# Three partition sums as fp32r products of a split, and a new order around the key-value product

## The chip, the cores and the metric

The kernel runs on one NeuronCore of a Trainium2 chip. The metric is device time in microseconds (us). Before the change it is 570.62 us, the median of three runs (570.37 to 571.47).

The core's engines each work through a queue of their own in order: TensorE (PE in the profile; PEld is its weight load) multiplies matrices into PSUM, VectorE (DVE) and ScalarE (ACT) do elementwise work, GpSimd (POOL) a little of it, and SyncE (SP) issues the DMA transfers. They wait for each other through semaphores.

## The reference

A transformer block with adaptive layer norm, on one sequence of S = 2048 tokens of width D = 512, in float32:

```python
mod = (silu(c) @ w_mod).reshape(1, 6, 1, D)
sa, ca, ga, sb, cb, gb = (mod[:, i] for i in range(6))

h = layernorm(x) * (1 + ca) + sa
q, k, v = heads(h @ wqkv)                 # 32 heads of 16
phi = lambda t: where(t > 0, t + 1, exp(t)) + 1e-6
kv = sum over tokens of phi(k) outer v    # 16 x 16 for each head
z  = sum over tokens of phi(k)
o  = (phi(q) @ kv) / (phi(q) . z + 1e-6)
x  = x + ga * (o @ wo)

h = layernorm(x) * (1 + cb) + sb
x = x + gb * (((h @ w_gate) * (h @ w_up)) @ w_down)   # inner width 1376
```

## The kernel before, in words

**Precision.** TensorE works on fp32r operands. To keep float32 accuracy, `split` writes an operand as two fp32r tiles: ScalarE copies the high part, VectorE subtracts it from the operand for the low part. `product` then adds three matmuls for each contraction block: high times high, high times low, low times high. Two kinds of matmul take plain fp32 operands instead: the transposes by an identity, and sums over partitions by a matrix or column of ones.

**Tiling.** Tokens come in 4 chunks (NCH) of 4 tiles (NJ) of 128; a tile is 128 x 512. Widths are cut into KD = 4 blocks of 128. All working tiles in SBUF come from one pool of 99 buffers. PSUM has eight banks of 128 x 512 fp32: four in the pool `ps_acc`, taken by `acc_bank()`, and four in `ps_w`, taken by `bank()`. A new tile of a pool takes a bank whose last reader in the program has read it.

**Order.** The order of each engine's queue is the order in which the program calls the instructions (`manual_schedule`, line 37); nothing reorders them. The stages are:

1. The modulation vectors ca and sa, the norm of the first chunk, the first key projections (to line 391).
2. The key loop (lines 421 to 469), 16 steps i. In step i TensorE makes a projection two tiles ahead (`proj`, 12 matmuls), and adds to `tacc`, four accumulated banks, the products of phi(k) with the normalized tokens (`t_tile`, 12 matmuls). ScalarE and VectorE split the tiles of step i + 1 and compute phi(k) of step i + 2. VectorE adds phi(k) into `zacc` (`z_add`). What else must be done goes into the steps by a table, `extra` (lines 405 to 418): splits of projection weights, DMA loads of `w_mod` (`mod_load`), the modulation vectors 2 to 5 as weighted sums on VectorE (`mod_part`), which then are summed over partitions. Vectors 2 (ga) and 5 (gb) become rows repeated on all partitions (`mod_row`, line 174, in steps 11 and 15); 3 and 4 become columns. In step 12 the four blocks of `wo` are loaded (`raw_o`), in step 14 they are split (`wo_s`). In the last step `zacc` is summed over partitions (line 464) and ScalarE writes `zb` from it.
3. The joint (lines 529 to 567). ScalarE and VectorE scale `tacc` (lines 535, 536) and split it into `tt`. TensorE makes `kvps`, the product of the value weights `wv` with `tt` (lines 543 to 546): 48 matmuls of 128 x 128 into one bank. VectorE masks it to its head blocks (line 553) into `kvf`, which is split into `kvp`. `w_out(g)` (line 517) multiplies block g of `kvp` with `wo_s[g]`, three matmuls into a new bank; VectorE multiplies by ga into f, and f is split into `wp[g]`. Between these stand q projections 6 to 10: `proj`, then `q_a` (Relu and Exp on ScalarE), then `q_b` on VectorE, which reads the projection's bank last. `den_z`, `den_a` (a multiplication with zb and a sum for each tile), `den_b` (an addition and a reciprocal for a chunk) and `den_c` give the denominators of phi(q), all on VectorE.
4. The attention output tile by tile (`turn_a`, `y_step`), the second norm, and the feed-forward: three of its eleven blocks at first in the plain way, then the rest in a scheme with seven products instead of eight (from `ffn`, line 972). The first feed-forward loads (`load_ffn`, line 651, called at line 732) follow the joint in the program. Their first users are the splits at line 1031.

The joint's order of calls before, as far as TensorE is concerned, is: q projections 6 and 7, `kvps`, q projections 8 and 9, w_out(0) to (3), q projection 10. The three sums over partitions are:

```python
nc.tensor.matmul(ps, ones, acc, start=True, stop=True)      # line 176, twice
nc.tensor.matmul(zps, ones, zacc, start=True, stop=True)    # line 464
```

Of the kernel before, what the change touches and what calls it, by code (L numbers as in the profile page):

```python
# [9 lines left out]
F32R = mybir.dt.float32r  # L10
# [4 lines left out]
P = 128  # L15
# [7 lines left out]
def tile_adaln_block(  # L23
# [12 lines left out]
    nc = tc.nc  # L36
# [23 lines left out]
    consts = pool("consts", 1)  # L60
# [10 lines left out]
    def T(p, tag, shape=(P, D), dt=F32, bufs=None):  # L71
        cnt[0] += 1
        return p.tile(list(shape), dt, tag="t" if p is tiles else tag, name=f"{tag}_{cnt[0]}", bufs=bufs)

    def B(tag, shape=(P, D), dt=F32):

        return T(tiles, tag, shape, dt)
# [4 lines left out]
    def bank():  # L82
        return T(ps_w, "bank")
# [6 lines left out]
    ones = consts.tile([P, P], F32, name="ones")  # L90
# [17 lines left out]
    def load(src, tag):  # L108
        raw = B(tag, (P, *src.shape[1:]))[:src.shape[0]]
        nc.sync.dma_start(raw, src)  # L110
        return raw
# [4 lines left out]
    def load_mod(v):  # L116
        return [load(wm_v[:, k, v * D:(v + 1) * D], "raw") for k in range(KD)]
# [18 lines left out]
    idle_f = B("f")  # L136
    nc.vector.memset(idle_f, 0.0)
    nc.vector.tensor_copy(idle, idle_f)
    ps_idle = T(ps_acc, "acc")

    def keep_on(n):
# [14 lines left out]
    def mod_acc(acc, raws, ks):  # L156
        for k in ks:
            if k == 0:
                nc.vector.tensor_scalar(acc, raws[k], sc[:, 0:1], None, op0=ALU.mult)
            else:  # L160
                nc.vector.scalar_tensor_tensor(acc, raws[k], sc[:, k:k + 1], acc, op0=ALU.mult, op1=ALU.add)

    def mod_col(acc, ps):

        for b in range(KD):
            nc.tensor.matmul(ps[:, b:b + 1], acc[:, b * P:(b + 1) * P], ones[:, 0:1], start=True, stop=True)
        return ps

    def col_out(v, ps, add):
        t = consts.tile([P, KD], F32, name=f"col{v}")  # L170
        nc.vector.tensor_scalar(t, ps[:, :KD], add, None, op0=ALU.add)
        return t

    def mod_row(v, acc):
        ps = bank()
        nc.tensor.matmul(ps, ones, acc, start=True, stop=True)
        t = consts.tile([P, D], F32, name=f"row{v}")
        nc.scalar.activation(t, ps, AF.Copy)
        return t


    def split(src, h, l, low=None):
        nc.scalar.activation(h, src, AF.Copy)  # L183
        (low or nc.vector).tensor_tensor(l, src, f32(h), op=ALU.subtract)  # L184

    def split_raw(raw, shape=(P, D), low=None):
        h = B("w", shape, F32R)
        l = B("w", shape, F32R)
        split(raw, h[:raw.shape[0]], l[:raw.shape[0]], low)
        return h, l  # L190

    def product(ps, pairs):

        n = len(pairs)
        for i, ((ah, al), (bh, bl)) in enumerate(pairs):
            nc.tensor.matmul(ps, ah, bh, start=i == 0, stop=False)  # L196
            nc.tensor.matmul(ps, ah, bl, start=False, stop=False)  # L197
            nc.tensor.matmul(ps, al, bh, start=False, stop=i == n - 1)  # L198
# [11 lines left out]
    def cut(pair, a, b):  # L210
        return pair[0][:, a:b], pair[1][:, a:b]
# [67 lines left out]
    wk, wq, wv = [], [], []  # L279
    kx, phk, phq, q_ps = {}, {}, {}, {}  # L280

    def proj(i, w, of=bank):

        ch, j = divmod(i, NJ)
        ps = of()
        product(ps, [(cut(norm[ch].t[k], j * P, (j + 1) * P), w[k]) for k in range(KD)])
        return ps

    def phi_a(ps, t):

        nc.scalar.activation(t, ps, AF.Relu, scale=-1.0)
        nc.scalar.activation(t, t, AF.Exp, scale=-1.0)

    def phi_b(ps, t):
        nc.vector.scalar_tensor_tensor(t, ps, 0.0, t, op0=ALU.max, op1=ALU.add)
# [35 lines left out]
    def q_a(i, ps):  # L331
        phq[i] = B("h")
        q_ps[i] = ps
        phi_a(ps, phq[i])

    def q_b(i):
        phi_b(q_ps.pop(i), phq[i])

    zacc = B("z")
# [52 lines left out]
    rows, cols = {}, {}  # L392
    accs = {}

    raw_m, raw_o, wo_s = {}, [], []

    def mod_load(*vs):
        raw_m.update({v: load_mod(v) for v in vs})

    def mod_part(v, *ks):  # L400
        if 0 in ks:
            accs[v] = B("f")
        mod_acc(accs[v], raw_m[v], ks)
# [6 lines left out]
             6: lambda: (wv.extend(split_raw(r) for r in raw_v[2:3]), mod_load(2),),  # L410
             7: lambda: (wv.extend(split_raw(r) for r in raw_v[3:4]),),
             8: lambda: (mod_part(2, 0, 1), mod_load(3)),
             9: lambda: (mod_part(2, 2, 3), mod_load(4)),
             10: lambda: (mod_part(3, 0, 1, 2), mod_load(5)),
             11: lambda: (mod_part(3, 3), mod_part(4, 0, 1), rows.update({2: mod_row(2, accs[2])})),
             12: lambda: (raw_o.extend(load(wo_v[k], "raw") for k in range(KD)), mod_part(4, 2, 3), cols.update({3: col_out(3, mod_col(accs[3], bank()), 0.0)})),
             13: lambda: (mod_part(5, 0, 1, 2), cols.update({4: col_out(4, mod_col(accs[4], bank()), 1.0)})),
             14: lambda: (mod_part(5, 3), wo_s.extend(split_raw(x) for x in raw_o)), 15: lambda: rows.update({5: mod_row(5, accs[5])})}
    q_at = {3: 0, 4: 1, 6: 2, 7: 3}
    ahead = {2: proj(2, wk)}  # L420
    for i in range(NT):
        ch, j = divmod(i, NJ)
        more = ch + 1 < NCH
        if i == 0:
            ahead[3] = proj(3, wk)
        elif i > 1:
            ahead[i + 2] = proj(i + 2, wk) if i + 2 < NT else proj(i + 6 - NT, wq)
        if i in q_at:
            qps = proj(q_at[i], wq)
        if more and j == 0:  # L430
            nx.xhat(2)
        if i + 1 < NT:
            k_split_x(i + 1)
        if more and j == 0:
            nx.xhat(3)
        if i + 1 < NT:
            k_split(i + 1)
        if more and j < 2:
            t_tile(i, 0, 1)
            nx.transpose(2 * j, 2 * j + 1)  # L440
            nx.modulated(ca, sa, 2 * j, 2 * j + 1, cast=nc.vector)
            norm[ch + 1:] = [nx]
        if ch + 2 < NCH and j == 2:
            nx2 = Norm(xts[ch + 2])
            nx2.stats(0, 1)
        if ch + 2 < NCH and j == 3:
            nx = nx2
            nx.stats(2, 3)
            nx.rstd_of()
            nx.nmr_of()  # L450
            nx.xhat(0, 1)
        if i + 2 < NT:
            k_phi(i + 2, ahead.pop(i + 2))
        else:
            q_a(i + 6 - NT, ahead.pop(i + 2))
            q_b(i + 6 - NT)
        if i in q_at:
            q_a(q_at[i], qps)
            q_b(q_at[i])
        if i + 1 < NT:  # L460
            z_add(i + 1)
        if i == NT - 1:
            zps = bank()
            nc.tensor.matmul(zps, ones, zacc, start=True, stop=True)
            zb = consts.tile([P, D], F32, name="zb")
            nc.scalar.activation(zb, zps, AF.Identity, bias=eps_z)
        t_tile(i, *range(2 if more and j < 2 else 0, KD))
        if i in extra:
            extra[i]()
# [8 lines left out]
    def den_z():  # L478

        nc.vector.reduce_sum(den0, zb.rearrange("p (h i) -> p h i", i=DH), axis=AX.X)  # L480
        nc.vector.tensor_scalar(den0, den0, EPS_PHI, EPS_DEN, op0=ALU.mult, op1=ALU.add)

    def den_p(ch, *js, on=None):
        for j in js:
            pzs[ch, j] = B("f")
            (on or nc.gpsimd).tensor_tensor(pzs[ch, j], phq[ch * NJ + j], zb, op=ALU.mult)

    def den_r(ch, *js):
        if ch not in dens:
            dens[ch] = T(small, "den", (P, NJ, NH))  # L490
        for j in js:
            nc.vector.reduce_sum(dens[ch][:, j], pzs.pop((ch, j)).rearrange("p (h i) -> p h i", i=DH), axis=AX.X)

    def den_a(ch, *js, on=None):

        for j in js:
            den_p(ch, j, on=on)
            den_r(ch, j)
# [13 lines left out]
    def q_tile(i):  # L512
        q_a(i, proj(i, wq))
# [12 lines left out]
            wp.append((B("w", dt=F32R), B("w", dt=F32R)))  # L526
            split(f, *wp[-1])

    den_z()
    den_a(0, 0, 1, on=nc.vector)  # L530
    ps = proj(6, wq)
    fs, tt = [], []
    for k in range(KD):
        f = B("n")
# [3 lines left out]
    for f in fs:  # L538
        tt.append((B("w", dt=F32R), B("w", dt=F32R)))
        split(f, *tt[-1])  # L540
    q_a(6, ps)
    q_tile(7)
    kvps = bank()
    for g in range(KD):
        a, b = g * P, (g + 1) * P
        product(kvps[:, a:b], [(cut(wv[k], a, b), cut(tt[k], a, b)) for k in range(KD)])
    q_b(6)
    q_b(7)
    den_a(0, 2, on=nc.vector)
    ps = proj(8, wq)  # L550
    kvp = (B("xh", dt=F32R), B("xl", dt=F32R))
    kvf = B("n")
    nc.vector.tensor_tensor(kvf.rearrange("p (g c) -> p g c", g=KD), kvps.rearrange("p (g c) -> p g c", g=KD),
                            mask.unsqueeze(1).to_broadcast([P, KD, P]), op=ALU.mult)
    den_p(0, 3, on=nc.vector)
    split(kvf, *kvp)
    den_r(0, 3)
    den_b(0)
    q_a(8, ps)
    ps = proj(9, wq)  # L560
    q_b(8)
    w_out(0, 1)
    q_a(9, ps)
# [457 lines left out]
    ps = proj(11, wq)  # L1021
# [176 lines left out]
```

## Time and profile before

| what | value |
|---|---|
| median of three runs | 570.62 us (570.37 to 571.47) |
| the profiled execution | 570.02 us, of which 568.3 us are span |
| VectorE, ScalarE, GpSimd busy | 373.1, 279.8, 186.2 us |
| the key loop's last product on TensorE | starts at 131.82 us |
| the key-value product | 138.38 to 143.81 us |
| w_out(0) to (3) on TensorE | 149.35 to 152.07 us |
| moved by DMA | 59.34 MB, 104 GB/s over the span |
| granted TensorE clock, mean | 0.999 |

The times of instructions are those of one profiled execution, from the first instruction of its span. In a timeline row stand the start, the duration, the engine, the line of the kernel, the operation, the written and the read tile and the shape; a count xN merges neighbours of one kind. In brackets stands how long the engine had been idle before the row and which engine and line released it. Matmuls overlap: one of 128 x 512 is shown with 0.39 us, and the next one begins 0.23 us after it. An fp32 matmul appears as two.

### The profile page before, as it was taken

What the parts mean: (1) busy time and instruction counts of PE and PEld (TensorE: products, weight loads), DVE (VectorE), ACT (ScalarE), POOL (GpSimd) and SP (SyncE); (2) the same over time, 40 slices, a digit from 0 to 9 for tenths busy, and PEclk for the clock granted to TensorE, in tenths of its full rate; (3) what the DMA queues carried; (4) which work ended last, traced back from release to release, by engine and by line L of the source; (5) the groups of instructions that cost most, each with busy time, mean ns of one, the idle gap of its engine ahead of it and who ended that gap; (6) DMA issues with size and microseconds to landing.
All of it is one profiled execution on the core that took longest, in us unless ns stands there. A gap on an engine that the chain in (4) does not pass through costs nothing.

```text
span 568.3 us, 7356 instructions
## 1 busy us (share of the span) xinstructions
PE 560.3 (99%) x2575; PEld 458.8 (81%) x2575; DVE 373.1 (66%) x614; ACT 279.8 (49%) x500; POOL 186.2 (33%) x191
## 2 busy tenths in 40 slices
PE   8999999999999999999989999999999999999997
PEld 6778888888888878878878888787888888888886
DVE  7876868868768876759767777745554434344445
ACT  3785857546456546445865545534333333334110
POOL 2000000000011300000579666665667446556200
PEclk9999999999999999999999999999999999999999
DMA  8900223302301000804208553599336012200004
GB/s 289 374 3 2 74 75 110 114 0 62 93 0 47 29 1 37 260 0 149 57 2 277 180 190 104 202 348 330 115 111 178 26 57 55 57 19 2 0 1 148
DMA packets 50309, 59.34 MB, mean 104 GB/s; under 512 B 6432, under 2 KB 27168, under 8 KB 50272
## 3 DMA queue, kind: packets, MB, share of 16 engines
q1 hardware_dynamic: 50272, 58.87, 32.1%
q8 instruction: 20, 0.33, 0.2%
q14 instruction: 17, 0.14, 0.1%
HBM read 43.12 MB, written 15.73 MB: 104 GB/s over the span
## 4 chain that ended last, share of the span: by engine, by line
PE 89%; DMA 3%; issue 2%; POOL 1%; DVE 1%; ACT 1%; SPq 1%; POOLq 0%; ACTq 0%
PE bank L838 28%; PE acc L914 6%; PE acc L915 6%; PE acc L916 6%; PE acc L614 6%; PE bank L198 5%; PE bank L196 5%; PE bank L197 5%; PE acc L329 3%; PE acc L327 3%; PE acc L328 3%; PE bank L693 2%; PE bank L691 2%; PE bank L692 2%; PE bank L250 2%
## 5 line engine op out<-in xcount | busy, mean ns | idle before, releaser
L838 PE MATMUL bank<-h,w 128*128 128x512 f32 (+1 forms) x798 | 185.5, 390 | 1.8 <-ACT bank L843 1.2
L838 PEld LDWEIGHTS bank<-h,w 128*128 128x128 f32 (+1 forms) x798 | 148.2, 186 | 35.3 <-ACT bank L843 1.7
L843 ACT ACTIVATE bank<-bank 128x512 f32<-128x512 f32 (+1 forms) x38 | 22.1, 583 | 144.8 <-PE bank L838 144.8
L678 DVE TENSOR_TENSOR x<-acc,x 128x512 f32<-128x512 f32 (+1 forms) x73 | 49.1, 684 | 49.0 <-PE acc L916 48.2
L824 POOL TENSOR_TENSOR w<-raw,w 128x256 fp32r<-128x256 f32 (+3 forms) x38 | 42.4, 1117 | 106.4 <-ACT w L817 86.4
L184 POOL TENSOR_TENSOR w<-raw,w 128x512 fp32r<-128x512 f32 (+1 forms) x25 | 34.9, 1399 | 116.0 <-DVE mv L226 87.6
L914 PE MATMUL acc<-w,kh 128*128 128x512 f32 (+2 forms) x154 | 59.6, 387 | 0.0
L915 PE MATMUL acc<-w,kh 128*128 128x512 f32 (+2 forms) x154 | 59.6, 387 | 0.0
L916 PE MATMUL acc<-w,kl 128*128 128x512 f32 (+2 forms) x154 | 59.5, 386 | 0.0
L234 POOL TENSOR_TENSOR rstd<-ve,half 128x4 f32<-128x4 f32 (+1 forms) x9 | 9.4, 1044 | 126.0 <-DVE ve L233 124.5
L184 DVE TENSOR_TENSOR kl<-u,kh 128x512 fp32r<-128x512 f32 (+1 forms) x38 | 26.8, 746 | 33.1 <-ACT kh L183 31.2
L824 POOL TENSOR_TENSOR w<-t,w 128x512 fp32r<-128x512 f32 (+1 forms) x38 | 48.4, 1293 | 0.0
L196 PE MATMUL bank<-w,h 128*128 128x512 f32 x112 | 45.0, 402 | 0.0
L198 PE MATMUL bank<-w,h 128*128 128x512 f32 x112 | 43.9, 392 | 0.0
L197 PE MATMUL bank<-w,h 128*128 128x512 f32 x112 | 43.6, 389 | 0.0
L614 PE MATMUL acc<-w,xh 128*128 128x512 f32 x120 | 38.1, 399 | 0.0
L914 PEld LDWEIGHTS acc<-w,kh 128*128 128x128 f32 (+1 forms) x154 | 28.9, 188 | 6.0
L916 PEld LDWEIGHTS acc<-w,kl 128*128 128x128 f32 (+1 forms) x154 | 28.9, 188 | 5.9
L915 PEld LDWEIGHTS acc<-w,kh 128*128 128x128 f32 (+1 forms) x154 | 28.9, 188 | 5.9
L893 DVE TENSOR_TENSOR u<-bank,u 128x512 f32<-128x512 f32 (+1 forms) x19 | 13.1, 690 | 30.0 <-PE bank L838 30.0
L243 ACT ACTIVATE n<-x,nmr,rstd 128x512 f32<-128x512 f32 x32 | 24.1, 804 | 17.2 <-DVE nmr L237 15.9
L262 ACT ACTIVATE f<-bank,col,col 128x512 f32<-128x512 f32 x28 | 20.7, 775 | 14.5 <-PE bank L250 12.4
(177 smaller groups left out, 1105.1 us busy)
## 6 DMA issues: line engine op xcount, KB each, us to landing
raw<-in_w_mod_dram SPq DMA_DIRECT2D x24, 256.0 KB, 3.7
raw<-in_B_w_down_dram SPq DMA_DIRECT2D x20, 256.0 KB, 2.9
raw<-in_B_w_gate_dram SPq DMA_DIRECT2D x36, 128.0 KB, 3.7
raw<-in_B_w_up_dram SPq DMA_DIRECT2D x36, 128.0 KB, 3.6
x<-in_A_x_dram SPq DMA_DIRECT2D x16, 256.0 KB, 5.4
kept<-f SPq DMA_DIRECT2D x16, 256.0 KB, 2.0
f<-kept SPq DMA_DIRECT2D x16, 256.0 KB, 4.8
side_s<-h SPq DMA_DIRECT2D x16, 256.0 KB, 2.6
```

The costliest lines, as they stand in the source:

```text
L184: (low or nc.vector).tensor_tensor(l, src, f32(h), op=ALU.subtract)
L196: nc.tensor.matmul(ps, ah, bh, start=i == 0, stop=False)
L197: nc.tensor.matmul(ps, ah, bl, start=False, stop=False)
L198: nc.tensor.matmul(ps, al, bh, start=False, stop=i == n - 1)
L243: nc.scalar.activation(self.n[j], self.tiles[j], AF.Identity, scale=self.rstd[:, j:j + 1], bias=self.nmr[:, j:j + 1])
L614: nc.tensor.matmul(yps[i], x, y, start=False, stop=k == KD - 1 and x is al, skip_group_check=True)
L678: nc.vector.tensor_tensor(xt[:, a:b], dn[j][:, a:b], xt[:, a:b], op=ALU.add)
L824: sub = lambda out, x, y: (on or nc.gpsimd).tensor_tensor(out, x, f32(y), op=ALU.subtract)
L838: mm = lambda x, y, **kw: nc.tensor.matmul(ps, x[:, k], y, skip_group_check=True, **kw)
L914: nc.tensor.matmul(ps, hh[:, a:b], dh[:n, c:d], start=i == 0, stop=False)
L915: nc.tensor.matmul(ps, hh[:, a:b], dl[:n, c:d], start=False, stop=False)
L916: nc.tensor.matmul(ps, hl[:, a:b], dh[:n, c:d], start=False, stop=i == len(hs) - 1)
```

## The change

A sum over partitions is now made by `column_sums`: two fp32r matmuls, with a matrix of ones in fp32r (`ones_r`, copied once by GpSimd), on the high and the low part of the summed tile. The three tiles are split ahead of it, in `extra`: `accs[2]` in step 9, `zacc` and `accs[5]` in step 14.

The four `wo` splits leave step 14. Two of them stand behind the 48 matmuls of `kvps` in the program, the other two behind `q_a(8)`. In the joint, `den_z` and the denominators of the first chunk's first two tiles move from ahead of q projection 6 to behind `kvps`; the tiles 2 and 3 of that chunk stand together in front of `den_b(0)`. TensorE's order becomes: q projections 6, 7 and 8, `kvps`, q projection 9, w_out(0) to (3), q projection 10.

The start of the kernel, the sums and the key loop:

```diff
     nc.vector.tensor_copy(idle, idle_f)
+    ones_r = consts.tile([P, P], F32R, name="ones_r")
+    nc.gpsimd.tensor_copy(ones_r, ones)
...
-    def mod_row(v, acc):
+    def column_sums(pair):
         ps = bank()
-        nc.tensor.matmul(ps, ones, acc, start=True, stop=True)
+        for i, x in enumerate(pair):
+            nc.tensor.matmul(ps, ones_r, x, start=i == 0, stop=i == 1)
+        return ps
+
+    def mod_row(v):
+        ps = column_sums(halves.pop(v))
         t = consts.tile([P, D], F32, name=f"row{v}")
         nc.scalar.activation(t, ps, AF.Copy)
         return t
+
+    halves = {}
...
-             9: lambda: (mod_part(2, 2, 3), mod_load(4)),
+             9: lambda: (mod_part(2, 2, 3), mod_load(4), halves.update({2: split_raw(accs[2])})),
...
-             11: lambda: (mod_part(3, 3), mod_part(4, 0, 1), rows.update({2: mod_row(2, accs[2])})),
+             11: lambda: (mod_part(3, 3), mod_part(4, 0, 1), rows.update({2: mod_row(2)})),
...
-             14: lambda: (mod_part(5, 3), wo_s.extend(split_raw(x) for x in raw_o)), 15: lambda: rows.update({5: mod_row(5, accs[5])})}
+             14: lambda: (halves.update({"z": split_raw(zacc)}), mod_part(5, 3), halves.update({5: split_raw(accs[5])})), 15: lambda: rows.update({5: mod_row(5)})}
...
         if i == NT - 1:
-            zps = bank()
-            nc.tensor.matmul(zps, ones, zacc, start=True, stop=True)
+            zps = column_sums(halves.pop("z"))
             zb = consts.tile([P, D], F32, name="zb")
```

The joint:

```diff
-    den_z()
-    den_a(0, 0, 1, on=nc.vector)
-    ps = proj(6, wq)
+    ps6 = proj(6, wq)
...
-    q_a(6, ps)
-    q_tile(7)
+    q_a(6, ps6)
+    ps7 = proj(7, wq)
+    q_a(7, ps7)
+    den_z()
+    q_b(6)
+    ps8 = proj(8, wq)
     kvps = bank()
     for g in range(KD):
         a, b = g * P, (g + 1) * P
         product(kvps[:, a:b], [(cut(wv[k], a, b), cut(tt[k], a, b)) for k in range(KD)])
-    q_b(6)
+    wo_s.extend(split_raw(x) for x in raw_o[:2])
     q_b(7)
-    den_a(0, 2, on=nc.vector)
-    ps = proj(8, wq)
+    den_a(0, 0, 1, on=nc.vector)
+    ps = proj(9, wq)
     kvp = (B("xh", dt=F32R), B("xl", dt=F32R))
     kvf = B("n")
     nc.vector.tensor_tensor(kvf.rearrange("p (g c) -> p g c", g=KD), kvps.rearrange("p (g c) -> p g c", g=KD),
                             mask.unsqueeze(1).to_broadcast([P, KD, P]), op=ALU.mult)
-    den_p(0, 3, on=nc.vector)
     split(kvf, *kvp)
-    den_r(0, 3)
+    q_a(8, ps8)
+    wo_s.extend(split_raw(x) for x in raw_o[2:])
+    den_a(0, 2, 3, on=nc.vector)
     den_b(0)
-    q_a(8, ps)
-    ps = proj(9, wq)
     q_b(8)
     w_out(0, 1)
     q_a(9, ps)
     den_c(0)
     w_out(2, 3)
     q_b(9)
     q_tile(10)
```

## The prediction

> **What bounds the kernel now.** I read the busy shares of the profile page first, then its chain of waits, then TensorE's own waits over the whole span.
>
> ```profile
> PE 560.3 (99%) x2575; PEld 458.8 (81%) x2575; DVE 373.1 (66%) x614; ACT 279.8 (49%) x500; POOL 186.2 (33%) x191
> PE 89%; DMA 3%; issue 2%; POOL 1%; DVE 1%; ACT 1%; SPq 1%; POOLq 0%; ACTq 0%
> ```
>
> TensorE is busy 99% of the span and carries 89% of the chain that ended last. Its waits, as engine, line waited for, releaser, total, times and longest, are few:
>
> ```profile
> PE acc L143 <- DVE w L138: 2.0, 1, 2.0
> PE bank L838 <- ACT bank L843: 1.2, 1, 1.2
> ```
>
> The first is the start of the kernel, the second lies in the last stage; between about 24 us and 232 us, where every edit lies, TensorE hardly waits. So a microsecond taken from TensorE's queue there is a microsecond of time, and so is a microsecond of new waiting. VectorE and ScalarE matter only where TensorE comes to need something they are late with. The question is therefore whether the new order hands TensorE everything in time.
>
> **The sums.** The timeline of TensorE (start us, us, engine, line, operation) shows two of the three sums and the single product matmul that follows the second one:
>
> ```profile
> 128.42 1.02 PE L464 MATMUL bank<-z,ones 128*128 128x512 f32 x2
> ...
> 132.04 1.02 PE L176 MATMUL bank<-f,ones 128*128 128x512 f32 x2
> ...
> 133.13 0.39 PE L197 MATMUL bank<-w,h 128*128 128x512 f32 x1
> ...
> 146.63 0.39 PE L196 MATMUL bank<-w,h 128*128 128x512 f32 x1
> ...
> 149.35 0.39 PE L196 MATMUL bank<-w,xh 128*128 128x512 f32 x1
> ```
>
> An fp32 sum is two passes. From its first pass at 132.04 to the second matmul after it at 133.13 are 1.09 us. An fp32r matmul of the same shape follows its predecessor after 0.227 us: the twelve of one q projection take 146.63 to 149.35, 2.72 us. Two fp32r passes and the one product then take 3 x 0.227 = 0.68 us. Each sum saves 1.09 - 0.68 = 0.41 us. All three stand in a queue that doesn't wait, so they save 3 x 0.41 = **1.2 us**.
>
> Each sum now needs a split of its input, one ScalarE copy and one VectorE subtraction. Three places must cover them:
>
> ```profile
> 98.27 1.53 DVE L161 SCALAR_TENSOR_TENSOR f<-raw,sc,f 128x512 f32<-128x512 f32 x2
> ...
> 103.86 0.39 PE L327 MATMUL acc<-kh,xh 128*128 128x512 f32 x1
> ...
> 125.09 0.68 DVE L312 TENSOR_TENSOR z<-z,phi 128x512 f32<-128x512 f32 x1
> ```
>
> In step 9 the ScalarE copy waits for the accumulation that ends at 98.27 + 1.53 = 99.80, and ScalarE's splits of the next key tile queue behind it. In chain: that copy (0.6), the normalized tile's high half (0.6), the key tile's (0.7), then VectorE's last subtraction (0.7) give about 102.5. The first user is the key-token product at 103.86, so over 1 us is spare. Were it gone, the cost would be the excess, microsecond for microsecond; I count 0.
>
> In step 14 the sum z is complete at 125.77. ScalarE copies it until 126.4, VectorE subtracts until 127.1, the last accumulation takes until 127.8, and the second split until about 129.3. The z sum would start at about 128.0 with the first 0.41 us already gained, the last sum at about 131.2. Both are covered by the q projection and the key-token products running meanwhile. I count 0, with 1 us or more in hand. The one GpSimd copy for ones_r runs in the first microseconds, where nothing needs GpSimd soon.
>
> **The reorder up to the key-value product.** Before, TensorE reaches it slightly too early:
>
> ```profile
> 139.34 0.28 PE L196 MATMUL bank<-w,w 128*128 128x128 f32 x1
> 139.52 0.33 PE L197 MATMUL bank<-w,w 128*128 128x128 f32 x1
> ...
> 143.81 0.44 PE L196 MATMUL bank<-w,h 128*128 128x512 f32 x1
> ```
>
> Among matmuls 0.11 us apart there is one gap of 0.18 us: 0.07 us of waiting for the last low half of tt. VectorE writes these, and ScalarE the high ones, here:
>
> ```profile
> 135.87 2.22 ACT L183 ACTIVATE w<-n 128x512 fp32r<-128x512 f32 x4
> 136.97 2.50 DVE L184 TENSOR_TENSOR w<-n,w 128x512 fp32r<-128x512 f32 x4
> ```
>
> Afterwards they come about 1.2 us earlier, since both follow the last sum, and TensorE comes 2.72 - 1.2 = 1.5 us later, with q projection 8 put ahead. The 0.07 us goes. Up to here the change has gained 1.28 us.
>
> The four wo splits leave step 14 (on ScalarE 2.18 us, on VectorE 2.49 us, rows below); nothing waits on them there, so their going gains nothing. Their inputs stay in SBUF some 20 us longer. The nine feed-forward loads compete for those buffers:
>
> ```profile
> 142.92 0.45 SPq L110 DMA_DIRECT2D raw<-in_B_w_down_dram  x1
> 166.51 1.15 ACT L183 ACTIVATE w<-raw 128x512 fp32r<-128x512 f32 x2
> ```
>
> The last of these leaves SyncE's queue at 142.92 and the first use of any is at 166.51. No DMA is moved or added, and even 10 us of lateness would be covered: 0.
>
> **What follows the key-value product.** Here a wait appears. The pool ps_w has four banks. When TensorE comes to w_out(2), they hold q projection 8 (until q_b(8) has read it), q projection 9 (until q_b(9)), w_out(0) and w_out(1) (each until VectorE's multiplication by ga). On VectorE all of these readers stand in the order q_b(8), w_out(0), w_out(1), ..., q_b(9). So w_out(2) can't start before **q_b(8)** is done. The same holds before, but there q_b(8) is early; after, VectorE must first do two wo subtractions, two multiply-and-sum pairs of the denominators and den_b, all of them behind the masking of the key-value product. First TensorE's own arrival:
>
> ```profile
> 150.71 0.39 PE L196 MATMUL bank<-w,xh 128*128 128x512 f32 x1
> ```
>
> That is w_out(2), now. The same matmuls precede it in both kernels, so it would be reached at 150.71 - 1.28 = 149.43. Now the lateness of q_b(8):
>
> ```profile
> 124.35 2.18 ACT L183 ACTIVATE w<-raw 128x512 fp32r<-128x512 f32 x4
> 144.74 0.63 ACT L183 ACTIVATE xh<-n 128x512 fp32r<-128x512 f32 x1 [4.36 <-DVE n L553]
> 146.83 0.60 ACT L291 ACTIVATE h<-bank 128x512 f32<-128x512 f32 x1 [1.45 <-PE bank L198]
> 147.46 0.63 ACT L292 ACTIVATE h<-h 128x512 f32<-128x512 f32 x1
> ```
> ```profile
> 126.35 2.49 DVE L184 TENSOR_TENSOR w<-raw,w 128x512 fp32r<-128x512 f32 x4
> 131.32 0.68 DVE L486 TENSOR_TENSOR f<-h,zb 128x512 f32<-128x512 f32 x1
> 132.04 0.69 DVE L492 TENSOR_REDUCE den<-f 128x32 f32<-128x512 f32 x1
> ...
> 144.02 0.69 DVE L553 TENSOR_TENSOR n<-bank,mask 128x512 f32<-128x512 f32 x1 [1.58 <-PE bank L198]
> ...
> 145.41 0.69 DVE L184 TENSOR_TENSOR xl<-n,xh 128x512 fp32r<-128x512 f32 x1
> ...
> 146.73 0.29 DVE L501 TENSOR_TENSOR den<-den,den 128x128 f32<-128x128 f32 x1
> 147.06 0.95 DVE L502 RECIPROCAL den<-den 128x128 f32<-128x128 f32 x1
> 148.12 0.69 DVE L295 SCALAR_TENSOR_TENSOR h<-bank,h 128x512 f32<-128x512 f32 x1
> ```
>
> The masking starts at 144.02 + 2.72 - 1.28 = 145.46. ScalarE begins the high half 0.72 later as now, 146.18; then Relu and Exp of q tile 8 at 146.72 and 147.35 (steps of 0.545 = 2.18 / 4, and 0.63 for the dependent one); then the two wo copies at 147.89 and 148.44. VectorE does the low half at 145.46 + 1.39 = 146.85, is done at 147.5 and waits: its next instruction is the subtraction of the third wo tile, whose copy ends at 147.89 + 0.6 = 148.49. From 148.5: two subtractions at 0.62 (2.49 / 4), to 149.74; two pairs at 0.72 + 0.61, to 152.40; the row above puts the addition 0.1 us behind that through the dependence, 152.49; the reciprocal 0.33 later and q_b(8) 1.06 after that, 153.88, done at 154.57. TensorE resumes at about 154.6.
>
> The stall is 154.6 - 149.43 = **5.2 us**. Its lower bound is the chain without the wait for ScalarE (1.0 us), 4.2 us; for the upper I allow another 0.5 us of hand-overs between the engines, 5.7 us. Behind the waiting matmul everything of TensorE is queued: w_out(3), q projection 10, the transposes, y. Next late would be the banks behind w_out:
>
> ```profile
> 150.23 1.37 DVE L523 TENSOR_TENSOR n<-bank,row 128x512 f32<-128x512 f32 x2 [1.41 <-PE bank L198]
> ...
> 153.51 1.28 DVE L523 TENSOR_TENSOR n<-bank,row 128x512 f32<-128x512 f32 x2
> ...
> 155.15 0.48 PE L196 MATMUL bank<-w,h 128*128 128x512 f32 x1
> ```
>
> VectorE's 150.23 moves to 154.49, by 4.26 us, while w_out(2) moves by 3.9 us. The nearest hand-over is w_out(3)'s bank to q projection 11: read out at 153.51 + 1.28 = 154.79, reused at 155.15. Its spare 0.36 us takes up the difference of 0.36 us, so no second stall of size follows.
>
> **The sum.** -1.21 (sums) - 0.07 (tt) + 5.2 (bank) = +3.9 us. The profiled execution took 570.02 us, 568.3 of it span; it becomes 573.9. The median of the three runs, 570.62, lies 0.6 above that execution, so I forecast 570.62 + 3.9 = **574.5 us**, with its own range 573.4 to 575.1 from the bounds of the stall (4.2 to 5.7) and 0.1 us for the hand-over behind it.
>
> **Rivals.**
>
> *The idle array comes back slow: 577.2 us.* The longest wait TensorE has inside the kernel is 1.2 us, so the trace doesn't show a resume after 5 us. What it does show is the start, after 2.0 us of idleness in the span and more ahead of it:
>
> ```profile
> 1.99 7.58 PE L143 MATMUL acc<-w 128*128 128x512 f32 x20 [1.99 <-DVE w L138]
> 15.85 2.34 PE L143 MATMUL acc<-w 128*128 128x512 f32 x9
> 2.00:4.00 2.00, 2.00 (x5) 1.61 (x6) 0.04 (x1) 0.07 (x1) 0.59 (x5) 1.00 0.74 261
> ```
>
> Twenty matmuls take 7.58 us, where at 0.227 us they would take 19 x 0.227 + 0.39 = 4.7; nine later ones take 2.34. The granted clock in the stretch from 2 to 4 us reads 1.00 (the number behind POOL's), so that column doesn't show the slowness; the spacing does. If a resume after 5 us behaves like the start, it costs up to 2.9 us; if like the waits of 1.2 us, nothing. 5 us is nearer to the start's idleness, yet that one is longer than the span shows, so I keep it as a rival of 2.7 us: 574.5 + 2.7 = 577.2. The Trainium skill, "TensorE: Matmul & The Clock Gate", Part 1, says that the array falls to half clock once a whole free-running window of about 3.4 us passed idle and recovers after a busy one. By that rule an idle stretch of 5 us holds such a window in some executions and not in others. Nothing in this trace tests it.
>
> *No stall: 569.3 us.* This one ends on the other side. It is one mechanism: the bank that w_out(2) takes is free when TensorE arrives at 149.4, and only the 1.28 us of gains is left. It decides by one comparison: whether q_b(8), or any reader of the other three banks, ends before 149.4. It would need VectorE's chain of 9.1 us from the masking to q_b(8) to shrink below 4.0 us, about what it takes now (144.02 to 148.12). For it speaks only that banks are given out by the program and not by me; against it the count of four live banks, and the order of VectorE's queue.
>
> *The sums gain nothing: 575.7 us.* If the two fp32r passes cost what two fp32 passes cost, 1.2 us of gain fails and the stall remains. Against it stand the fp32r matmuls of the same shape at 0.227 us.
>
> **How the numbers follow.** Forecast 0.50, slow resume 0.34, no stall 0.10, sums without gain 0.06. The forecast, the slow resume and the third rival are all slower. The range reaches from 573.0 to 577.6 and leaves out the no-stall case and a little at each edge. A measurement of this kernel tells about 0.2%, 1.1 us, from no change. The no-stall case at -1.28 us stands at that edge, so its 0.10 is halved: faster 0.05, same 0.05, slower 0.90.
>
> **What would show it.** Right: the sums as two matmuls at the usual spacing; tt without the gap at the start of the key-value product; TensorE idle for about 5 us in front of the third product of w_out, released by VectorE's q_b(8) on line 295's operation; VectorE's chain of about 9 us ahead of it; everything later by about 3.9 us. Wrong: w_out's four products in one unbroken row, or a stall whose releaser is a wo split or the low half of kvp, or matmuls about 0.4 us apart behind the stall, which would be the slow resume.

## The result, and the profile after

The changed kernel takes 576.01 us (median of six runs, 574.53 to 576.34); the kernel before, beside it, 570.50. The ratio is 1.0093, with a 95% interval of 1.0079 to 1.0108: slower by 5.5 us. The profiled execution took 576.19 us against 570.02 before.

The busy shares and the chain of waits of the changed kernel:

```profile
PE 561.4 (98%) x2575; PEld 460.2 (80%) x2575; DVE 374.7 (65%) x617; ACT 281.1 (49%) x503; POOL 185.9 (32%) x192
PE 87%; DMA 4%; issue 3%; DVE 2%; ACT 1%; POOL 1%; SPq 1%; POOLq 0%
```

TensorE's share of the chain falls by two points while its own work hardly changes: it waits more. Its waits (engine, line waited for, releaser, total, times, longest) name the place; lines are those of the changed kernel, where L205 to L207 are `product` and L304 is `phi_b`, the instruction of `q_b`:

```profile
PE bank L205 <- DVE h L304: 4.8, 1, 4.8
PE acc L145 <- DVE w L138: 2.0, 1, 2.0
```

One new wait of 4.8 us, released by a `q_b`. In TensorE's timeline (start, duration, engine, line, operation):

```profile
128.26 0.63 PE L179 MATMUL bank<-w,ones_r 128*128 128x512 f32 x2
...
131.47 0.63 PE L179 MATMUL bank<-w,ones_r 128*128 128x512 f32 x2
131.94 0.39 PE L205 MATMUL bank<-w,h 128*128 128x512 f32 x1
...
149.40 0.39 PE L207 MATMUL bank<-w,xl 128*128 128x512 f32 x1
154.64 0.77 PE L205 MATMUL bank<-w,xh 128*128 128x512 f32 x1 [4.85 <-DVE h L304]
155.20 0.63 PE L206 MATMUL bank<-w,xh 128*128 128x512 f32 x1
155.63 0.63 PE L207 MATMUL bank<-w,xl 128*128 128x512 f32 x1
...
160.32 0.52 PE L206 MATMUL bank<-w,h 128*128 128x512 f32 x1
160.68 0.40 PE L207 MATMUL bank<-w,h 128*128 128x512 f32 x1
```

Three things stand there. The sums are cheap: from the z sum to the last sum are 3.21 us, where before they were 132.04 - 128.42 = 3.62. The third product of w_out follows the second by 5.24 us instead of 0.23. And behind the stall the matmuls come 0.43 us apart until 160.3; the 14 steps from 154.64 to 160.68 take 6.04 us instead of 14 x 0.227 = 3.18, 2.9 us more. The windows of that stretch (window, its length, busy time and count of PE, PEld, DVE, ACT and POOL, then the granted clock) show why:

```profile
149.00:152.00 3.00, 0.79 (x4) 0.33 (x2) 2.93 (x6) 0.18 (x1) 0.00 (x0) 1.00 0.24 62
152.00:154.60 2.60, 0.00 (x0) 0.00 (x0) 2.53 (x5) 0.00 (x0) 0.00 (x0) 0.84 0.00 0
154.60:157.00 2.40, 2.36 (x6) 1.91 (x7) 2.30 (x5) 1.85 (x4) 0.00 (x0) 0.50 0.00 0
157.00:160.50 3.50, 3.50 (x10) 2.73 (x9) 3.40 (x7) 1.73 (x3) 0.00 (x0) 0.50 0.02 5
160.50:164.00 3.50, 3.50 (x19) 2.89 (x18) 1.39 (x3) 2.17 (x4) 0.00 (x0) 0.99 0.00 0
```

The clock falls to half late in the idle stretch and stays there for six microseconds of work. VectorE is busy nearly throughout the stall. (`den_z`, told above as moved behind `kvps`, stands ahead of it, between `q_a(7)` and `q_b(6)`; it is not part of this chain.) Its chain, with ScalarE's two rows that it waits for:

```profile
146.36 0.63 ACT L192 ACTIVATE xh<-n 128x512 fp32r<-128x512 f32 x1 [5.89 <-DVE n L563]
...
148.05 1.13 ACT L192 ACTIVATE w<-raw 128x512 fp32r<-128x512 f32 x2
```
```profile
145.64 0.69 DVE L563 TENSOR_TENSOR n<-bank,mask 128x512 f32<-128x512 f32 x1 [1.12 <-PE bank L207]
147.03 0.69 DVE L193 TENSOR_TENSOR xl<-n,xh 128x512 fp32r<-128x512 f32 x1 [0.70 <-ACT xh L192]
148.70 1.29 DVE L193 TENSOR_TENSOR w<-raw,w 128x512 fp32r<-128x512 f32 x2 [0.98 <-ACT w L192]
149.91 0.68 DVE L494 TENSOR_TENSOR f<-h,zb 128x512 f32<-128x512 f32 x1
...
152.99 0.95 DVE L510 RECIPROCAL den<-den 128x128 f32<-128x128 f32 x1
153.86 0.63 DVE L304 SCALAR_TENSOR_TENSOR h<-bank,h 128x512 f32<-128x512 f32 x1
```

The masking starts at 145.64, the wo subtractions at 148.70 after almost 1 us of waiting for ScalarE. Two denominators and the reciprocal follow, and q_b(8) runs from 153.86 to 154.49. TensorE resumes at 154.64.

### The profile page after: what moved, and what is told of

Read it like the earlier page. It is cut to its first block, busy times and chain, and to the rows that moved or that the text cites. A ratio compares the mean times of both kernels' runs of the same rounds, so it can differ in the third digit from the quotient of the medians.

```text
span 574.5 us, 7359 instructions
## 1 busy us (share of the span) xinstructions
PE 561.4 (98%) x2575; PEld 460.2 (80%) x2575; DVE 374.7 (65%) x617; ACT 281.1 (49%) x503; POOL 185.9 (32%) x192
## 4 chain that ended last, share of the span: by engine, by line
PE 87%; DMA 4%; issue 3%; DVE 2%; ACT 1%; POOL 1%; SPq 1%; POOLq 0%
PE bank L847 29%; PE acc L923 6%; PE acc L924 6%; PE acc L925 6%; PE acc L623 6%; PE bank L205 4%; PE bank L207 4%; PE bank L206 4%; PE acc L338 3%; PE acc L337 3%; PE acc L336 3%; PE bank L702 2%; PE bank L700 2%; PE bank L701 2%; PE bank L259 2%
## 5 line engine op out<-in xcount | busy, mean ns | idle before, releaser
L205 PE MATMUL bank<-w,h 128*128 128x512 f32 x112 | 44.8, 400 | 0.0
L207 PE MATMUL bank<-w,h 128*128 128x512 f32 x112 | 44.4, 396 | 0.0
L192 ACT ACTIVATE w<-raw 128x512 fp32r<-128x512 f32 (+2 forms) x44 | 26.5, 617 | 2.8 <-DMA raw<-in_A_wqkv_dram 1.9
```

## The experiments

**Sums alone.** The sums as in the change; the joint, up to w_out(0, 1), in the lines of the kernel before. Against the changed kernel, besides the joint:

```diff
-             13: lambda: (mod_part(5, 0, 1, 2), cols.update({4: col_out(4, mod_col(accs[4], bank()), 1.0)})),
+             13: lambda: (mod_part(5, 0, 1, 2), cols.update({4: col_out(4, mod_col(accs[4], bank()), 1.0)}), wo_s.extend(split_raw(x) for x in raw_o)),
```

> The three sums as split fp32r products, with the joint in the order of before; the wo splits move from step 14 to step 13 of the key loop, where ScalarE and VectorE wait longest. Theory (the sums gain, the new order of the joint loses): about 569.3 us, 1.2 us below before, TensorE without a wait in the joint. Rival (the added splits hold up the key loop, and the loss lies there): 570.5 us or more, with waits of TensorE in steps 9 to 15.

Measured: 569.68 us (568.39 to 572.13, eleven runs) against 570.20, ratio 0.9991 (0.9980 to 1.0002): no difference that stands clear of the noise. The trace has no wait in the key loop, so the rival falls; but of the 1.2 us less than half shows between the medians. The key-value product of this kernel:

```profile
137.82 0.27 PE L205 MATMUL bank<-w,w 128*128 128x128 f32 x1
138.14 0.33 PE L206 MATMUL bank<-w,w 128*128 128x128 f32 x1
...
138.42 0.27 PE L205 MATMUL bank<-w,w 128*128 128x128 f32 x1
138.75 0.33 PE L206 MATMUL bank<-w,w 128*128 128x128 f32 x1
...
139.02 0.27 PE L205 MATMUL bank<-w,w 128*128 128x128 f32 x1
139.35 0.33 PE L206 MATMUL bank<-w,w 128*128 128x128 f32 x1
```

Where steps of 0.11 us are usual stand three of 0.32: 0.65 us of waiting for the low halves of tt. VectorE comes to tt hardly earlier than before (134.15 us against 134.31), since two denominators stand ahead:

```profile
134.15 2.73 DVE L544 SCALAR_TENSOR_TENSOR n<-zb,col,n 128x512 f32<-128x512 f32 x4
```

No wait stands in front of this row: VectorE went straight from the denominators to tt. So the cheaper sums need some change of the joint's order, or TensorE merely waits there.

**Order alone.** The kernel before with the new joint and the fp32 sums; against it, besides the joint of the change:

```diff
-             14: lambda: (mod_part(5, 3), wo_s.extend(split_raw(x) for x in raw_o)), 15: lambda: rows.update({5: mod_row(5, accs[5])})}
+             14: lambda: (mod_part(5, 3)), 15: lambda: rows.update({5: mod_row(5, accs[5])})}
```

> The new joint with the fp32 sums of before. Theory: the wait for q_b(8) is as long as in the changed kernel, since the masking of the key-value product shifts with TensorE; 1.2 us above the changed kernel, about 577.2 us. Rival (the wait comes from TensorE arriving early, thanks to the cheaper sums): a wait shorter by 1.2 us and a time like the changed kernel's, 576.0 us or less.

Measured: 576.69 us, ratio 1.0107 (1.0092 to 1.0122), and again a wait of 4.8 us for `q_b`. The wait doesn't depend on the sums. The order alone loses what the change loses; between the two medians the sums make up some 0.7 us of the 1.2 expected.

**The idle stretch filled.**

```diff
     den_c(0)
+    ps_fill = acc_bank()
+    for _ in range(20):
+        nc.tensor.matmul(ps_fill, wq[0][0][:, :P], wq[0][0], start=True, stop=True)
     w_out(2, 3)
```

> The changed kernel with 20 more fp32r matmuls into a bank of their own in front of w_out(2), 20 x 0.227 = 4.5 us of work whose result nobody reads, where TensorE otherwise idles. Theory (the idle array comes back slow and that alone makes the 13 matmuls 0.43 us apart): these come back at 0.23 us, and the time falls by 13 x 0.2 = 2.6 us for the executions that have them, to about 573.5 to 574.5 us. Rival (the slow matmuls come from what runs beside them on the other engines): they stay, 576.0 us.

Measured: 573.29 us, ratio 1.0051 (1.0037 to 1.0064), 2.7 us below the changed kernel. The bank comes free when it did (in this execution the whole joint stands 0.5 us earlier), and the matmuls behind it follow at full speed (first matmul after the fill, and the next):

```profile
149.14 4.69 PE L576 MATMUL acc<-w 128*128 128x512 f32 x20
154.16 0.47 PE L205 MATMUL bank<-w,xh 128*128 128x512 f32 x1 [0.32 <-DVE h L304]
154.46 0.40 PE L206 MATMUL bank<-w,xh 128*128 128x512 f32 x1
```

So the slow stretch comes from TensorE's idleness alone. The loss of 5.5 us is thereby split: 2.8 us of it are the stall less the gains (3.1 against the kernel before as run beside the filled one, 570.20), 2.7 us the slow clock.

**q_b(8) earlier.**

```diff
     q_a(8, ps8)
+    q_b(8)
     wo_s.extend(split_raw(x) for x in raw_o[2:])
     den_a(0, 2, 3, on=nc.vector)
     den_b(0)
-    q_b(8)
```

> The changed kernel with q_b(8) right behind q_a(8), ahead of the last two wo splits and the denominators. Theory (VectorE's whole queue behind the masking is late, the bank of q projection 8 is only the first to show it): w_out(2) starts at once, and w_out(3) waits for VectorE's reading of w_out(0), until about 154.5; the gain is 0.7 to 0.9 us, about 575.2 us. Rival (the place of q_b(8) alone makes the wait): no wait left, about 569.3 us.

Measured: 574.20 us, ratio 1.0064 (1.0050 to 1.0077). The wait has moved, as expected, to the fourth product, which waits for VectorE's reading of the first (L531):

```profile
PE bank L205 <- DVE n L531: 4.2, 1, 4.2
```

The gain is 1.8 us instead of 0.7 to 0.9. The idle stretch is shorter by 0.6 us, and the profiled execution has six or seven slow matmuls instead of thirteen. The rival falls: all of VectorE's queue is late, not one instruction of it.

**The wo splits out of the joint.** The changed kernel with all four splits in step 13, by the line shown under the sums alone, and:

```diff
-    wo_s.extend(split_raw(x) for x in raw_o[:2])
     q_b(7)
...
     q_a(8, ps8)
-    wo_s.extend(split_raw(x) for x in raw_o[2:])
     den_a(0, 2, 3, on=nc.vector)
```

> The changed kernel with all four wo splits in step 13 of the key loop instead of the joint; the rest of the joint stays. Theory (VectorE's chain from the masking to q_b(8) sets the wait): the chain loses two subtractions (1.24 us) and the wait for ScalarE's copies (1.0 us), the stall shrinks from 5.0 to about 2.7 us; at least 2.2 us gained, 573.8 us, and 2.6 us more, 571.2 us, if so short an idleness doesn't slow the array. Rival (the denominators alone set the wait): a stall near 5 us, 576.0 us.

Measured: 572.08 us (570.82 to 573.65, eight runs), ratio 1.0031 (1.0020 to 1.0042). The wait is 2.5 us long, so the wo splits made 2.4 us of it. The rest has two parts that no run separates: the denominators behind the masking, and q projection 8, which now stands ahead of `kvps` and makes the masking later. TensorE would reach w_out(2) 6.69 us after the masking's start before (150.71 - 144.02), and only 3.99 us after it here (149.93 - 145.94). The time falls between the two forecasts, and the runs form two groups: three with a mean clock of 1.000 at 570.82 to 571.56 us, five with 0.996 or 0.997 at 572.03 to 573.65. The profiled execution is of the second group:

```profile
152.58 0.50 PE L205 MATMUL bank<-w,xh 128*128 128x512 f32 x1 [2.48 <-DVE h L304]
152.92 0.40 PE L206 MATMUL bank<-w,xh 128*128 128x512 f32 x1
153.16 0.40 PE L207 MATMUL bank<-w,xl 128*128 128x512 f32 x1
153.39 0.49 PE L205 MATMUL bank<-w,xh 128*128 128x512 f32 x1
153.68 0.63 PE L206 MATMUL bank<-w,xh 128*128 128x512 f32 x1
154.11 0.63 PE L207 MATMUL bank<-w,xl 128*128 128x512 f32 x1
```

TensorE resumes at full speed and turns slow 0.8 us later, for eight matmuls.

**How much idleness slows the array.** The filled kernel with fewer idle matmuls, 8 in one and 13 in the other:

```diff
-    for _ in range(20):
+    for _ in range(8):
```

> The filled kernel with 8 instead of 20 idle matmuls, so that TensorE idles for 0.3 + 12 x 0.227 = 3.0 us in front of w_out(2). The wait itself ends at the same time. Theory (it takes a whole window of about 3.4 us of idleness to slow the array, by the clock-gate rule): no slow matmuls in any execution, 573.3 us as with 20. Rival (a shorter idleness or a share of a window is enough): matmuls 0.43 us apart behind the wait in some or all executions, up to 576.0 us.

> The filled kernel with 13 idle matmuls, so that TensorE idles for 0.3 + 7 x 0.227 = 1.9 us in front of w_out(2). Theory (what slows the array is a window mostly idle, 2.5 us were enough): 1.9 us of 3.4 is too little, no slow matmuls, 573.3 us as with 20. Rival (any idleness of a few tenths of a window is enough): matmuls 0.43 us apart behind the wait, 574 to 575 us.

Measured: 574.97 us with 8 (574.68 to 575.32 in four runs), ratio 1.0085 (1.0070 to 1.0099); 573.50 us with 13 (573.11 to 573.83 in four), ratio 1.0053 (1.0039 to 1.0067). The first rows behind the wait, with 8 and with 13:

```profile
154.33 0.77 PE L205 MATMUL bank<-w,xh 128*128 128x512 f32 x1 [3.03 <-DVE h L304]
154.90 0.63 PE L206 MATMUL bank<-w,xh 128*128 128x512 f32 x1
155.32 0.63 PE L207 MATMUL bank<-w,xl 128*128 128x512 f32 x1
```
```profile
154.24 0.47 PE L205 MATMUL bank<-w,xh 128*128 128x512 f32 x1 [1.90 <-DVE h L304]
154.55 0.39 PE L206 MATMUL bank<-w,xh 128*128 128x512 f32 x1
154.78 0.40 PE L207 MATMUL bank<-w,xl 128*128 128x512 f32 x1
```

After 3.0 us of idleness the array was slow, and all four times lie about 1.7 us above those of the full fill. After 1.9 us it wasn't, in none of four runs (mean clock 0.999 or 1.000). The theory for 8 falls; that for 13 stands.

**The best version.** The sums alone, with the denominators of tile 1 behind the key-value product. Against the sums alone:

```diff
     den_z()
-    den_a(0, 0, 1, on=nc.vector)
+    den_a(0, 0, on=nc.vector)
     ps = proj(6, wq)
...
     q_b(7)
-    den_a(0, 2, on=nc.vector)
+    den_a(0, 1, 2, on=nc.vector)
     ps = proj(8, wq)
```

> The kernel with the sums alone, and the denominators of tile 1 moved from ahead of tt to behind q_b(7), where VectorE idled for 1.96 us. Theory (the sums bring TensorE to the key-value product before tt is ready, three gaps of 0.22 us there, since tt stands behind VectorE's denominators): the gaps go, tt begins some 0.7 us earlier, and the time is 0.6 to 0.7 us below that kernel's, about 569.0 us, 1.2 to 1.3 us below before. Rival (tt is bound by ScalarE, or the masking becomes late): the gaps stay or a wait comes at w_out, no gain against the sums alone.

Measured: 568.33 us (567.85 to 569.39), ratio 0.9968 (0.9956 to 0.9980): faster than before by 1.9 us, and than the changed kernel by 7.7. Against the sums alone it is 1.35 us, twice the forecast. In the traces the move at tt is worth 0.7 us of this; another 0.7 us is a wait at 306 us, in the feed-forward, which of these two only the trace of the sums alone has. VectorE now comes to tt early enough to wait for ScalarE, and of the three gaps one of 0.20 us is left:

```profile
133.13 2.74 DVE L544 SCALAR_TENSOR_TENSOR n<-zb,col,n 128x512 f32<-128x512 f32 x4 [0.56 <-ACT n L543]
```
```profile
138.14 0.28 PE L205 MATMUL bank<-w,w 128*128 128x128 f32 x1
138.34 0.33 PE L206 MATMUL bank<-w,w 128*128 128x128 f32 x1
```

**Its moves alone.** The kernel before with the same two moves, its fp32 sums kept:

```diff
-             13: lambda: (mod_part(5, 0, 1, 2), cols.update({4: col_out(4, mod_col(accs[4], bank()), 1.0)})),
-             14: lambda: (mod_part(5, 3), wo_s.extend(split_raw(x) for x in raw_o)), 15: lambda: rows.update({5: mod_row(5, accs[5])})}
+             13: lambda: (mod_part(5, 0, 1, 2), cols.update({4: col_out(4, mod_col(accs[4], bank()), 1.0)}), wo_s.extend(split_raw(x) for x in raw_o)),
+             14: lambda: (mod_part(5, 3)), 15: lambda: rows.update({5: mod_row(5, accs[5])})}
...
-    den_a(0, 0, 1, on=nc.vector)
+    den_a(0, 0, on=nc.vector)
...
-    den_a(0, 2, on=nc.vector)
+    den_a(0, 1, 2, on=nc.vector)
```

> The kernel before with fp32 sums, and only the two moves of the best version: the wo splits in step 13, the denominators of tile 1 behind q_b(7). Theory (the moves only keep the gain of the sums from being lost): 0.07 us of waiting for tt is all that they can gain, 570.1 to 570.3 us, no difference. Rival (the moves themselves gain what the best version has beyond the 1.2 us of the sums): 0.5 to 0.7 us below before.

Measured: 570.00 us against 570.36, ratio 0.9989 (0.9980 to 0.9998). A gain of 0.1 to 1.1 us, more than the 0.07 us that I could name. The traces show where it lies: not in the joint. Matched matmul by matmul, this kernel's TensorE is 0.04 to 0.10 us ahead of the kernel before from the end of the key loop to 366 us, and 0.62 to 0.66 us ahead from 367 us on. At that place, in the feed-forward, TensorE of the kernel before waits for VectorE's reading of a bank, which this kernel's doesn't; before, then this run:

```profile
366.77 1.42 PE L838 MATMUL bank<-h,w 128*128 128x512 f32 x5 [0.28 <-DVE u L893]
```
```profile
365.11 2.67 PE L838 MATMUL bank<-h,w 128*128 128x512 f32 x11
```

None of the other traces has a wait at this place. Why it goes, and whether it stands in every execution of the kernel before, isn't shown. With the 1.2 us of the sums the gain makes up the 1.9 us of the best version within the intervals.

## Why the prediction was right, and what it mis-sized

- **The bound.** Right: TensorE's queue sets the end, and each microsecond of its waiting in the joint came out at the end.
- **The sums.** Right: 0.41 us each (three times that are 1.23, where the prediction adds 1.21). The splits in steps 9 and 14 caused no wait.
- **tt.** Right for the changed kernel, whose key-value product begins at the usual spacing. What the prediction didn't see is what the reorder is good for: without it the earlier TensorE waits 0.65 us for tt (sums alone).
- **The bank of q projection 8.** Right in place, releaser and size. q_b(8) was forecast from 153.88 to 154.57 and ran from 153.86 to 154.49; TensorE was to resume at 154.6 and did at 154.64; the stall of 5.2 us was one of 5.0 (5.24 from matmul to matmul, less 0.23). That q_b(8) came within 0.02 us is partly luck: the masking began 0.18 us later than forecast, and the chain from there was 0.20 us shorter. The order alone and the earlier q_b(8) show that neither the sums nor the one instruction makes the stall, and the kernel without wo splits in the joint that these are worth 2.4 us of it.
- **The slow resume.** Here the sum went wrong: it counted 0 for it and left it as a rival of 2.7 us at 0.34. The trace of before offered two rows, the waits of 1.2 us without a slow clock and the start with it; the text even found 5 us nearer to the start, and then took the value of the other row. The filled kernel shows that the term belongs in the sum: 2.7 us. One of the prediction's own signs of being wrong, matmuls about 0.4 us apart behind the stall, came true. Five of the six runs lie at 575.8 to 576.3, and one, with a mean clock of 0.997 instead of 0.993 or 0.994, at 574.53. That this is the forecast's 574.5 is chance: 0.997 is also the clock of the traces with 3.4 us at half speed, so this run most likely had a slow resume too, a shorter one.
- **The rest.** Forecast with the rival's term: 577.2; measured 576.0. Some 1 us is missing, and the filled kernel (573.29 where the sum says 574.2) and the best version (568.33 for 569.0) also come out 0.7 to 0.9 us below such sums. Of this, 0.55 us can be placed in the traces: it is the wait at 366.77 us that the kernel before has in the feed-forward and that is in no other trace here. The prediction counted no change so far behind the joint. All of these kernels have the wo splits taken out of step 14, but that alone is no cause of a gain: the sums alone have it too and come out at their sum (570.20 - 1.2 + 0.65 is 569.65, measured 569.68), with another such wait, at 306 us. The cause stays open, and so does the rest of the 1 us. The gain that is missing from the sum works against the slow resume that is missing too, so the forecast came closer than its terms.

## What to carry to other kernels

An engine that is busy 99% can still lose to the order of another one's queue: when work is moved behind a product, ask which PSUM bank its last reader frees, and what is queued ahead of that reader. Price a stall of the tensor engine with its slow resume, not by its length alone; if it can't be avoided, matmuls whose result nobody reads, put into the gap, kept the clock here and did not lengthen the wait. A gain on the bound engine shows only if what feeds it next is moved forward by as much.

## What the runs showed of the hardware

The clock falls after shorter idleness than I had expected: idle stretches of 5.0 and 3.0 us slowed the array in the profiled executions, one of 2.5 us slowed it 0.8 us after work had resumed (by the mean clock in five of eight executions), one of 1.9 us not at all in four, which is at most 56% of the 3.41 us below. The Trainium skill, "TensorE: Matmul & The Clock Gate", Part 1, asks for at least one whole window of about 3.4 us passed idle. Against that stand the 3.0 and the 2.5 us here: a window mostly idle was enough.

How full such a window was can be read from the traces. From its first change on, the granted clock changes only at whole multiples of 3.413 us: in the changed kernel's trace it is full for 146.77 us, half for 6.83, full for 413.01, which are 43, 2 and 121 times that. Cut at these points, the trace with 2.5 us of idleness reads, ahead of the fall and behind it:

```profile
150.13:153.54 3.41, 0.96 (x4) 0.82 (x5) 3.34 (x6) 0.39 (x1) 0.00 (x0) 1.00 0.00 0
153.54:156.95 3.41, 3.41 (x10) 2.66 (x9) 3.27 (x6) 2.56 (x6) 0.00 (x0) 0.50 0.00 0
```

TensorE worked for 0.96 us of the window that ended with the fall, and was idle for 2.45. In the trace of the order alone even 2.23 idle microseconds of the 3.41 were enough. So it matters where the idleness lies against these windows, and executions of one kernel differ.

The cost isn't fixed: 13 slow matmuls in the changed kernel's profiled execution, six or seven with q_b(8) earlier and with 8 idle matmuls, eight after 2.5 us. The same cut shows one reason. With q_b(8) earlier TensorE works for 2.81 us of the first slow window, and the clock is full behind it; in the changed kernel it works for 2.52 us of it, and a second slow window follows. At the start of the span the matmuls are slow as well, with a granted clock that reads 1.00; in the stall's stretch it reads 0.50. So the column can be trusted here in the middle of the span, not at its start.
